# A new order for a fused attention and two-layer MLP kernel: additions placed clear of GpSimd's maxima, small transfers issued by ScalarE

## Chip, cores, metric

One core of one Trainium2 chip. The time is device microseconds of one launch; lower is better. Inputs lie in HBM, the output goes to HBM.

## What is computed

Causal attention over 4 batches x 12 heads x 448 positions x 64 dims, then an MLP on the 1792 x 768 result:

```python
scores = scale * np.matmul(q, k.transpose(0, 1, 3, 2))
scores = np.where(mask, -1000000000.0, scores)
scores = scores - np.max(scores, axis=-1, keepdims=True)
attn = np.exp(scores)
attn = attn / (np.sum(attn, axis=-1, keepdims=True) + 1e-09)
x = np.matmul(attn, v)                   # (4, 12, 448, 64)
x = x.transpose(0, 2, 1, 3).reshape(1792, 768)
h = x @ w_in                             # 768 x 2048
return np.maximum(0.01 * h, h) @ w_out   # 2048 x 768
```

The weights arrive as float64 and are unpacked to float32 on the chip.

## The kernel before

**Attention** runs in 24 units of two heads. For a unit, `qk_load` and `v_load` (issued by SyncE, SP) bring q, k and v; TensorE transposes them (`features`, L421; from unit 12 on VectorE does it, L413), and multiplies keys by queries (`scores`, L450, and the causal mask, L464). A score tile has keys on partitions, so the maximum of softmax runs over partitions: `head` copies chunk 0 to `M` (ScalarE, L479), VectorE takes three elementwise maxima (L264, `M<-S,M`), GpSimd the maximum over partitions (L484, `partition_all_reduce`), VectorE subtracts it chunk by chunk (L489), ScalarE takes the exponential (L496). `products` multiplies by v (L508) and copies the result to `xu` (L514).

**Every second unit `finish` divides.** From batch 1 on VectorE first adds the chunks of each head (three additions `t<-t` per head at L264, turn "add", 108 in all). TensorE sums over keys (L528), ScalarE copies the sums (`sr`, L540), a DMA `sc<-sr` spreads them over 112 partitions ("spread"), VectorE adds 1e-9 and inverts (L543, L544), a DMA `scr<-rc` stores them to HBM ("store"), four DMAs `rb<-scr` broadcast them ("broadcast", issued by ScalarE), and VectorE multiplies (`rb<-xu,rb` or `xf<-xu,rb`) and, for batches 0 and 1, splits x into two parts (ScalarE L261, VectorE `xt<-rb,xt`).

**The MLP.** `layer1` (L602) multiplies batches 0 and 1 by w_in in 576 matmuls; it can start once the x of batch 0 (units 0 to 5) is there, and TensorE weaves it into the attention of later units. Its results go through ScalarE (L607) into one of two buffers `h` and by SP to HBM (`gd<-h`). The weights are unpacked meanwhile: `stage<-in_moe_w_in_dram` by SP, L348, L350 and L370 on ScalarE, L352 and L372 on VectorE. During batches 2 and 3 `ahead` unpacks half of w_out in the same way. After attention `layer1_pair` (L796) and `layer2` (L983) run on TensorE alone.

**Order.** Every operation is recorded with a turn (table `TURN`, one number per kind and unit) and a supposed duration. `Plan.emit` lists them: it takes the engine that is free first, and on it the ready operation with the least turn. The list only sets the order on each engine; the waits on the chip follow from the tiles. Each engine's queue runs in that order, a DMA issue included: an issue that waits holds back all that stands behind it on the engine. Where the plan sees TensorE free it puts warm-up matmuls (L337).

Of the kernel before, what the change touches and what calls it, by code (L numbers as in the profile page):

```python
# [21 lines left out]
    "add": [25.6, 26.6, 27.6, 28.6, 29.6, 30.6, 31.6, 1602.8, 33.6, 1848.1, 35.6, 1480.5, 37.6, 1711.9, 39.6, 1657.6, 41.6, 1656.3, 43.6, 1475.8, 45.6, 1555.1, 47.6, 1436.2],  # L22
    "load": [-2261.1, -2171.6, -2129.4, -2294.2, -2241.4, -2008.9, -1959.9, -1993.3, -1930.3, -2037.5, -2195, -2231.3, -2282, -2312.8, -2224.5, -2161.3, -2231.8, -2175.5, -2242.8, -2255.7, -2117.3, -1991.7, -2075.3, -2074.3],
    "v": [608.6, 652.5, 523.1, 637.8, 734.3, 703.2, 762.6, 586.3, 552.7, 540.9, 645.9, 708.1, 594.1, 649.7, 683.3, 857.5, 861.1, 731.2, 722.3, 719.3, 478.6, 398.8, 556.5, 637.8],
    "transpose": [816, 712.2, 714.5, 763.8, 784.7, 940, 977.5, 999.9, 1298.3, 1281.2, 1210.2, 1393.4, 120.9, 121.9, 122.9, 123.9, 124.9, 125.9, 126.9, 127.9, 128.9, 129.9, 130.9, 131.9],
    "features": [355.5, 270.7, 175.8, 197.8, 329.8, 157.7, 322.1, 351, 391.4, 565.4, 502.8, 597.8, 725.5, 522.1, 546.6, 623, 382.1, 371, 458.7, 236.6, 182.1, 183.3, 171.6, 412.4],
    "scores": [-2016.4, -1926.5, -1879.1, -1903.1, -1875.5, -1837.1, -1727.3, -1731.1, -1837, -1813.4, -1690.1, -1795, -1711.2, -1757.4, -1696.1, -1800.5, -1952.8, -1827, -1903.7, -1725.1, -1882.4, -1895.5, -1928.5, -1800.7],
    "chunk 0": [284.7, 252.5, 434, 449, 448.3, 219.8, 302.8, 386.7, 273.1, 256.8, 189, 193.7, 234.8, 108.9, 159.3, 80, 116.4, -84.5, 28.7, 206.5, 203.1, 222.8, 121, 304.9],
    "max": [-442.1, -415.1, -493, -637, -572.2, -486.9, -543, -585.1, -461.8, -558, -566.8, -672.6, -686.1, -734.9, -552.2, -601.7, -501.7, -450.3, -531.8, -542.6, -594.7, -629.6, -469.8, -416.7],
    "all max": [-1401.3, -1500.2, -1321.8, -1250.4, -1245.6, -1456.8, -1308.5, -1187.8, -1316.5, -1389.6, -1406.9, -1359.6, -1351.7, -1354.9, -1452, -1392.8, -1305.4, -1489.4, -1243.8, -1368.1, -1251.4, -1197.9, -1268.1, -1364.1],  # L30
    "subtract": [3.3, 57.3, 150.1, 102.4, 14.2, 78.1, -59.8, 5.3, 52.2, 67.2, 20.3, 51.6, -222.9, -12.4, -115.4, -84.4, 142.9, 97.4, 198.6, 263.3, 69.9, 170.2, 72.8, 86.1],
    "exp": [-710.2, -914.1, -824.3, -918.4, -801.6, -725.9, -641, -658.2, -777.6, -973.2, -956.7, -1017.4, -1169.2, -1033.8, -996.6, -1022.3, -1081, -957.1, -785.9, -837.9, -834.8, -837.6, -844.2, -736.1],
    "products": [504.4, 609.8, 417.8, 630.3, 514.2, 280.5, 326.3, 302.8, 441.2, 524, 338.2, 416.9, 400.4, 290.3, 306.1, 479.9, 449.6, 568, 460.4, 565.9, 520.1, 509.8, 631.3, 441.2],
# [9 lines left out]
    "out": [140.9, 31.9, -18.1, 33.6, -14, 25.5, 14, 44, 122, 189.5, 211, 171.3, -14.1, 11.2, -68.9, 43.6],
    "xs": [10645.3, 10569.2, 10738.1, 10680.2, 10711.9, 10841.8, 10757.6, 10751.2, 10924, 10924.4, 10920],
    "pair": [10852, 10998.1, 10978, 11043.4, 11022.1, 11050.1, 11075.8, 11360.1],
    "rows": [10737.1, 10610.6, 10696.8, 10778.6, 10751.4, 10772.2, 10635.9, 10692.9, 10658.9, 10721.5, 10679.8, 10681, 10648.9, 10472.9, 10405, 10446.5],
    "product": [-447.4, -613.4, -574.8, -599.2, -666.7, -724.4, -752.5],
    "x lo": [219.3, -457.4, 221.3, -333.8, 223.3, -742.8, 225.3, -349.3, 227.3, -323.9, 229.3, -426, 231.3, -389.5, 233.3, -231.9, 235.3, -265.4, 237.3, -259.8, 239.3, -219.7, 241.3, -253.6],
# [8 lines left out]
PIECE = [1736.3, 1759.7, 1688.7, 1587.5, 1386.6, 1565.0, 1459.4, 1626.7, 1500.3, 1410.5, 1612.2, 1692.9, 1723.9, 1726.6, 1579.9, 1568.4]  # L57


SAME = -365.86  # L60


class Plan:
# [32 lines left out]
    def emit(self, slack, filler):  # L96
# [36 lines left out]
        for _ in range(n):  # L133
# [42 lines left out]
def attention_moe_kernel(  # L176
# [15 lines left out]
    nc = tc.nc  # L192
# [238 lines left out]
    def scores(u):  # L431
# [37 lines left out]
        for e in range(2):  # L469
            head(2 * u + e, e, sl)  # L470
# [607 lines left out]
```

## Time and profile before

| | |
|---|---|
| median of 3 runs | 591.46 us (589.79 to 592.78) |
| the profiled execution | 590.4 us, span 588.6 us |
| TensorE busy | 570.9 us (97%) |
| VectorE busy | 499.6 us (85%) |
| ScalarE busy | 327.8 us (56%) |
| GpSimd busy | 80.5 us (14%) |
| HBM read, written | 99.09 MB, 26.56 MB |

The profile is one execution. PE is TensorE, PEld its weight load, DVE VectorE, ACT ScalarE, POOL GpSimd, SP SyncE; SPq and ACTq are DMA issues on those engines. Busy times of neighbouring instructions on one engine overlap a little, so an engine can be at its limit somewhat below the length of a window.

### The profile page before, as it was taken

Reading aid. Unit: us, or ns where it says so; the run is one execution under the profiler, and the core shown is the slowest. Engines: PE = TensorE matmul, PEld = TensorE weight load, DVE = VectorE, ACT = ScalarE, POOL = GpSimd, SP = SyncE. Lnnn points to the kernel's source line nnn. Section 1 sums busy time; section 2 is a strip of 40 time slices with the busy share of each in tenths; the row PEclk is TensorE's granted clock in tenths of the full one; section 3 lists DMA queues with packets and bytes.
Section 4 is the critical chain, followed back from the end, with each engine's and each line's share of the span. In section 5 each row is a group of like instructions: output and inputs, shape, how many; then the busy total and the mean of one; then the engine's idle time right before and its main releaser. Section 6 shows DMA issues by size and latency. Waiting matters only on the chain.

```text
span 588.6 us, 10664 instructions
## 1 busy us (share of the span) xinstructions
PE 570.9 (97%) x3602; PEld 494.1 (84%) x3602; DVE 499.6 (85%) x1044; ACT 327.8 (56%) x560; POOL 80.5 (14%) x54
## 2 busy tenths in 40 slices
PE   7998899999999999999999999999999999999997
PEld 6666567677777767689999899999999999999997
DVE  4798999999988988966987899899988897888872
ACT  3987797676545666634545775555455544333320
POOL 2443424222423222400000000000000000000000
PEclk9998999999999999999999999999999999999999
DMA  8998678875667898432136996999999997887761
GB/s 174 257 243 193 159 151 253 229 191 122 141 138 199 210 274 257 147 97 94 48 117 203 323 367 219 297 329 303 317 275 281 280 293 202 246 256 230 237 187 52
DMA packets 208967, 126.46 MB, mean 215 GB/s; under 512 B 98832, under 2 KB 202768, under 8 KB 208912
## 3 DMA queue, kind: packets, MB, share of 16 engines
q1 hardware_dynamic: 205072, 120.27, 72.8%
q10 hardware_dynamic: 3840, 5.51, 3.2%
q8 instruction: 28, 0.46, 0.3%
q14 instruction: 27, 0.22, 0.1%
HBM read 99.09 MB, written 26.56 MB: 213 GB/s over the span
## 4 chain that ended last, share of the span: by engine, by line
PE 69%; DMA 12%; DVE 9%; ACT 6%; issue 2%; SPq 2%; POOL 0%; ACTq 0%; DVEq 0%
PE h L983 34%; PE h L796 14%; PE h L602 12%; PE S L450 4%; PE big L508 3%; DMA rb<-scr 2%; DVE t L489 2%; DMA wo<-spare 2%; SPq L258 2%; DMA raw<-in_k_dram 2%; DMA ahead<-in_moe_w_out_dram 1%; DVE t L264 1%; DMA wo<-ahead 1%; ACT t L496 1%; DMA words<-in_moe_w_out_dram 1%
## 5 line engine op out<-in xcount | busy, mean ns | idle before, releaser
L983 PE MATMUL h<-W,r 128*128 128x384 f32 x696 | 127.5, 335 | 0.2
L602 PE MATMUL h<-xt,w 128*128 128x448 f32 x576 | 125.9, 372 | 1.7 <-ACT h L607 1.4
L983 PEld LDWEIGHTS h<-W,r 128*128 128x128 f32 x696 | 121.1, 188 | 0.9 <-ACT r L654 0.4
L602 PEld LDWEIGHTS h<-xt,w 128*128 128x128 f32 x576 | 105.7, 188 | 18.1 <-issue 5.9
L484 POOL PARTITION_ALL_REDUCE MR<-M x48 | 79.9, 1713 | 167.6 <-DVE M L264 120.9
L983 PE MATMUL h<-W,raws 128*128 128x384 f32 x480 | 89.5, 334 | 0.0
L983 PEld LDWEIGHTS h<-W,raws 128*128 128x128 f32 x480 | 83.8, 188 | 0.0
L489 DVE TENSOR_TENSOR t<-S,MR 128x64 f32<-128x64 f32 x192 | 67.6, 415 | 2.0 <-POOL MR L484 1.8
L496 ACT ACTIVATE t<-t 128x1024 f32<-128x1024 f32 x48 | 50.7, 1058 | 18.0 <-DVE t L489 13.3
L264 DVE TENSOR_TENSOR M<-S,M 128x320 f32<-128x320 f32 x144 | 49.1, 353 | 12.6 <-PE S L464 7.2
L450 PE MATMUL S<-kq 64*128 64x64 f32 (+3 forms) x384 | 58.2, 414 | 1.6 <-DVE t L489 1.6
L450 PEld LDWEIGHTS S<-kq 64*128 64x128 f32 x384 | 36.7, 191 | 21.1 <-issue 16.1
L508 PE MATMUL big<-t,v 128*64 128x448 f32 (+3 forms) x384 | 47.2, 386 | 3.5 <-ACT sr L540 1.8
L508 PEld LDWEIGHTS big<-t,v 128*64 128x64 f32 x384 | 26.7, 136 | 25.1 <-issue 10.5
L652 DVE TENSOR_TENSOR v<-A 128x512 f32<-128x512 f32 x70 | 46.6, 694 | 0.0
L654 ACT ACTIVATE r<-v 128x512 fp32r<-128x512 f32 x41 | 24.6, 600 | 37.5 <-DVE v L652 30.6
L264 DVE TENSOR_TENSOR t<-t 128x64 f32<-128x64 f32 (+2 forms) x108 | 39.3, 375 | 2.4 <-PE big L508 0.5
L1011 DVE TENSOR_TENSOR C<-C,h 128x384 f32<-128x384 f32 x56 | 29.1, 550 | 13.3 <-PE h L983 13.3
L655 DVE TENSOR_TENSOR r<-v,r 128x512 fp32r<-128x512 f32 x41 | 28.2, 689 | 8.9 <-ACT r L654 7.6
L654 ACT ACTIVATE W<-v 128x384 fp32r<-128x384 f32 x40 | 19.6, 489 | 27.3 <-DVE v L652 25.0
L654 ACT ACTIVATE raws<-v 128x512 fp32r<-128x512 f32 x29 | 17.4, 601 | 25.6 <-DVE v L652 23.6
L796 PE MATMUL h<-xs,w 128*128 128x448 f32 x144 | 31.6, 366 | 0.0
(108 smaller groups left out, 791.9 us busy)
## 6 DMA issues: line engine op xcount, KB each, us to landing
A<-gd SPq DMA_DIRECT2D x126, 256.0 KB, 4.8
stage<-in_moe_w_in_dram SPq DMA_DIRECT2D x16, 768.0 KB
val<-wo SPq DMA_DIRECT2D x64, 192.0 KB, 4.4
gd<-h SPq DMA_DIRECT2D x51, 224.0 KB, 2.1
ahead<-in_moe_w_out_dram SPq DMA_DIRECT2D x16, 384.0 KB, 4.3
words<-in_moe_w_out_dram SPq DMA_DIRECT2D x16, 384.0 KB, 4.5
val<-wo SPq DMA_DIRECT2D x16, 384.0 KB, 5.3
rb<-scr ACTq DMA_DIRECT2D x48, 112.0 KB, 3.1
```

What stands on the lines that cost most here:

```text
L264: return dve(n, lambda: nc.vector.tensor_tensor(out=out_(), in0=a(), in1=b(), op=op), r, w, prio, **kw)
L450: nc.tensor.matmul(out=T[S_, 2 * e + bank][:, col:col + n], lhsT=T[kq][rows, 128 * c:128 * c + 128], rhs=T[kq][rows, S + qs:2 * S], start= ...
L484: P.op("Pool", 1.75, both(new(mr, p1, [128, S], F32, f"MR{g % 2}"), lambda: nc.gpsimd.partition_all_reduce(T[mr], T[m], 128, ReduceOp.max) ...
L489: f = lambda c=c, qs=qs, n=n: nc.vector.tensor_tensor(out=T[t][:, at(c):at(c) + n], in0=s(c), in1=T[mr][:, qs:], op=ALU.subtract)
L496: act(1024 + 55, lambda: nc.scalar.activation(out=T[t], in_=T[t], func=ACTF.Exp, scale=scale), (), [t], turn("exp", u))
L508: nc.tensor.matmul(out=bigs(key[1])[64 * e:64 * e + 64, qs:S], lhsT=T[vv][:, c, e, :], rhs=T["t", (2 * u + e) % NTB][:, 512 * bank + col:5 ...
L602: nc.tensor.matmul(out=T[key][:, :S], lhsT=T[w, f, 1][:, 128 * c:128 * c + 128], rhs=T["xt", b, x // 3][:, x % 3], start=(c == 0 and j == ...
L652: nc.vector.tensor_tensor(out=x(), in0=get(terms[0]), in1=get(terms[1]), op=ALU.add if terms[2] > 0 else ALU.subtract)
L654: act(n, lambda: nc.scalar.activation(out=hi(), in_=x(), func=ACTF.Copy), [*rd, *hold], [(out_cell, "h")], prio)
L796: nc.tensor.matmul(out=T[key[1]][:, :S], lhsT=wt(o, c), rhs=T["X", x, h][c] if x == "B11" else T["X", x, h][:, c], start=start and c == 0 ...
L983: nc.tensor.matmul(out=T[key][:, :HO], lhsT=g()[:, jj * 128:jj * 128 + 128], rhs=W[:, w * HO:(w + 1) * HO], start=(e == 0 and jj == 0 and ...
L1011: dve(HO, lambda C=C, x=x, sign=sign: nc.vector.tensor_tensor(out=T[C], in0=T[C], in1=x(), op=ALU.add if sign > 0 else ALU.subtract), (), ...
```

## The change

The table of turns is new throughout, and so are `PIECE` and `SAME`. The plan's model is changed: an operation of VectorE that has both inputs in SBUF (marked `cfg=1`) is supposed to shut out GpSimd's maximum and be shut out by it, gets a penalty of 400 in its turn while one runs, and SP's queue is supposed to hold 6.5 us of transfers. Dependencies are recorded per chunk. "spread" and "store" are issued by ScalarE instead of SP, as are the first two q loads; a one-element exponential at the start loads ScalarE's table. Nothing of what is computed changes.

```diff
-    "add": [25.6, 26.6, 27.6, 28.6, 29.6, 30.6, 31.6, 1602.8, 33.6, 1848.1, 35.6, 1480.5, 37.6, 1711.9, 39.6, 1657.6, 41.6, 1656.3, 43.6, 1475.8, 45.6, 1555.1, 47.6, 1436.2],
+    "add": [25.6, 26.6, 27.6, 28.6, 29.6, 30.6, 31.6, 1710.2, 33.6, 1946.1, 35.6, 1528.8, 37.6, 1946.6, 39.6, 1947.6, 41.6, 1955.7, 43.6, 1723.5, 45.6, 1893.7, 47.6, 1693],
...
-SAME = -365.86
+SAME = 384.58
+
+
+DEEP = 6.5
+
+LOCKP = 400
...
-                    key=lambda i: (ops[i][4] - (self.SAME if e == "PE" and ops[i][9] == split else 0.0), i))
+                    key=lambda i: (ops[i][4] - (self.SAME if e == "PE" and ops[i][9] == split else 0.0)
+                                   + (LOCKP if e == "DVE" and ops[i][9] and lock[0] <= t < lock[1] else 0.0), i))
...
+                if e == "DVE" and cfg:
+                    if lock[0] <= t < lock[1]:
+                        t = lock[1]
+                    port = t + us
                 end = free[e] = t + us
+                if e == "Pool" and us > 1:
+                    lock = t + 0.2, max(t + 0.2, port) + 0.74
+                    end = free[e] = lock[1] + 0.7
             if late:
                 dma = max(dma, end + 1.5) + late
+                if e == "SP":
+                    free[e] = max(end, dma - DEEP)
...
+    P.op("ACT", 1.4, lambda: nc.scalar.activation(out=early, in_=ones[:, 0:1], func=ACTF.Exp), ("ones",), ("early",), FIRST)
...
-                loaded[u, tag] = dma(400, lambda key=key: T[key],
-                                     lambda src=src: src[b, 2 * p:2 * p + 2].rearrange("h (s c) d -> s c h d", c=4), [key], [(*key, 0)], turn("load", u))
+                loaded[u, tag] = dma(420, lambda key=key: T[key],
+                                     lambda src=src: src[b, 2 * p:2 * p + 2].rearrange("h (s c) d -> s c h d", c=4), [key], [(*key, 0)], turn("load", u),
+                                     *((0.47, "ACT") if u < 2 and j else ()))
...
-                   (), [("t", g % NTB)], turn("add", u), chain=0.02)
+                   (), [("t", g % NTB)], turn("add", u), cfg=1)
...
-        dma(7, lambda: T[sc], lambda: T[sr][0:97:32, :].rearrange("o (p j) -> o p j", j=16), [sr], [sc], turn("spread", u), 0.68)
+        dma(7, lambda: T[sc], lambda: T[sr][0:97:32, :].rearrange("o (p j) -> o p j", j=16), [sr], [sc], turn("spread", u), 0.53, eng="ACT")
...
-        dma(7, lambda: scr.rearrange("a (p j) -> (a p) j", j=16), lambda: T[rc], [rc], [("scr", u)], turn("store", u))
+        dma(7, lambda: scr.rearrange("a (p j) -> (a p) j", j=16), lambda: T[rc], [rc], [("scr", u)], turn("store", u), 0.53, eng="ACT")
...
-        P.emit({"PE": 0.1, "DVE": 0.1, "ACT": 0.1}, (0.029, "tp", warm))
+        P.emit({"PE": 0.1, "DVE": 0.03, "ACT": 0.1}, (0.029, "tp", warm))
```

What this makes of the order is seen on the engines, at three places. L273 of the changed kernel is L258 of the one before (a DMA), L279 is L264, L512 is L489, L369 is L352.

**The first transfers.** SP's queue before; then SP's and ScalarE's with the change. `raw0` and `raw1` take k and q of even and odd units, `stage` a piece of w_in.

```order
L258 DMA raw0_91<-in_k_dram 112x8x64
L258 DMA raw0_91<-in_q_dram 112x8x64
L258 DMA raw1_93<-in_k_dram 112x8x64
L258 DMA raw1_93<-in_q_dram 112x8x64
L258 DMA v0_92<-in_v_dram 128x3x64 x2
L258 DMA v0_92<-in_v_dram 64x2x64
L258 DMA v1_94<-in_v_dram 128x3x64 x2
L258 DMA raw0_91<-in_k_dram 112x8x64
L258 DMA raw0_91<-in_q_dram 112x8x64
```

```order
L273 DMA raw0_92<-in_k_dram 112x8x64
L273 DMA raw1_94<-in_k_dram 112x8x64
L273 DMA v1_95<-in_v_dram 128x3x64 x2
L273 DMA v1_95<-in_v_dram 64x2x64
L273 DMA v0_93<-in_v_dram 128x3x64 x2
L273 DMA v0_93<-in_v_dram 64x2x64
L273 DMA raw0_92<-in_k_dram 112x8x64
L273 DMA stage_119<-in_moe_w_in_dram 128x6x256
L273 DMA raw0_92<-in_q_dram 112x8x64
```

```order
L273 DMA raw0_92<-in_q_dram 112x8x64
L273 DMA raw1_94<-in_q_dram 112x8x64
L316 ACT_TABLE_LOAD
L316 ACTIVATE early_89<-ones_87 128x1
L443 ACTIVATE kq_0_132<-big_90 128x448
```

The k of unit 1 is now SP's second transfer, not its third; q of units 0 and 1 are ScalarE's first; the first piece of w_in goes ahead of the q of unit 2.

**ScalarE's queue at the second division** (units 2 and 3; `sr` holds the sums). With the change, from the issue of "spread" to the first "broadcast":

```order
L273 DMA sc_0_120<-sr_0_769 112x1x16
L498 ACTIVATE M_1_797<-S_711 128x448
L517 ACTIVATE t_3_606<-t_3_606 128x1024
L367 ACTIVATE stage_119<-stage_119 128x768
L536 ACTIVATE xu_0_817<-big_91 128x448
...
L273 DMA scr3_99<-rc_0_860 112x16
L498 ACTIVATE M_1_874<-S_803 128x448
L517 ACTIVATE t_4_767<-t_4_767 128x1024
L517 ACTIVATE t_5_768<-t_5_768 128x1024
L443 ACTIVATE kq_0_906<-big_90 128x448
L387 ACTIVATE w_908<-stage_119 128x768
L273 DMA rb_0_121<-scr3_99 64x448 x2
```

Before, the first and the seventh of these rows stood in SP's queue, and ScalarE's had M, two exponentials and one kq ahead of the broadcasts. Now both wait and are waited for in ScalarE's own queue.

**VectorE's queue in batch 3**, from the last subtractions of one unit to the first of the next; first before, then with the change:

```order
L264 TENSOR_TENSOR M_0_2604<-S_2571,M_0_2604 128x320
L264 TENSOR_TENSOR M_0_2604<-S_2571,M_0_2604 128x192
L264 TENSOR_TENSOR M_0_2604<-S_2569,M_0_2604 128x64
L264 TENSOR_TENSOR M_1_2608<-S_2572,M_1_2608 128x320
L264 TENSOR_TENSOR M_1_2608<-S_2572,M_1_2608 128x192
L264 TENSOR_TENSOR M_1_2608<-S_2570,M_1_2608 128x64
L352 SCALAR_TENSOR_TENSOR ahead_2267<-ahead_2267,ahead_2266 128x384
L264 TENSOR_TENSOR t_2_2518<-t_2_2518 128x64
L352 SCALAR_TENSOR_TENSOR spare1_96<-spare1_96,spare0_95 128x384
L543 TENSOR_SCALAR sc_0_116<-sc_0_116 112x16
L544 RECIPROCAL rc_0_2646<-sc_0_116 112x16
L489 TENSOR_TENSOR t_4_2654<-S_2569,MR_0_2622 128x64
```

```order
L279 TENSOR_TENSOR M_0_2681<-S_2645,M_0_2681 128x320
L279 TENSOR_TENSOR M_0_2681<-S_2645,M_0_2681 128x192
L369 SCALAR_TENSOR_TENSOR spare1_97<-spare1_97,spare0_96 128x384
L279 TENSOR_TENSOR M_0_2681<-S_2643,M_0_2681 128x64
L279 TENSOR_TENSOR M_1_2689<-S_2646,M_1_2689 128x320
L279 TENSOR_TENSOR t_2_2554<-t_2_2554 128x64
L279 TENSOR_TENSOR M_1_2689<-S_2646,M_1_2689 128x192
L279 TENSOR_TENSOR t_2_2554<-t_2_2554 128x192
L279 TENSOR_TENSOR M_1_2689<-S_2644,M_1_2689 128x64
L512 TENSOR_TENSOR t_4_2552<-S_2643,MR_0_2705 128x64
```

Before, an addition and two unpackings stood between the last maximum of both heads and the first subtraction; now one unpacking stands ahead of M_0's last maximum, and the additions among the maxima of the second head.

## Rows read from the trace of the kernel before

**Rows 1.** Busy time in stretches of core 0: stretch, length, engines, clock, DMA.

```profile
0.00:20.00 20.00, 16.74 (x211) 13.33 (x213) 10.25 (x43) 10.39 (x16) 4.39 (x9) 1.00 0.92 207
20.00:45.00 25.00, 23.23 (x228) 15.46 (x224) 23.14 (x58) 22.44 (x37) 12.48 (x8) 1.00 1.01 242
45.00:70.00 25.00, 19.95 (x166) 13.22 (x165) 21.94 (x56) 18.72 (x30) 10.08 (x6) 0.93 0.70 153
70.00:100.00 30.00, 30.00 (x215) 21.85 (x214) 28.63 (x68) 26.45 (x40) 7.18 (x6) 1.00 0.86 220
100.00:125.00 25.00, 24.53 (x153) 18.07 (x153) 24.04 (x54) 17.36 (x25) 6.50 (x4) 1.00 0.86 232
125.00:200.00 75.00, 74.93 (x519) 55.54 (x515) 68.50 (x180) 42.42 (x70) 23.07 (x14) 1.00 0.65 153
200.00:250.00 50.00, 47.52 (x311) 35.86 (x308) 43.14 (x113) 32.20 (x58) 16.77 (x10) 1.00 0.77 224
```

**Rows 2.** The chain that ended last: start us, us, what.

```profile
259.83 16.93 PE h L602 x81
...
276.76 40.32 PE h L796 x198
```

**Rows 3.** Timeline, 0 to 20 us: start, us, engine, line, operation, idle before.

```profile
2.24 0.69 SPq L258 DMA_DIRECT2D raw<-in_k_dram  x1
...
12.06 0.60 PE L421 MATMUL big<-ident,raw 112*128 112x112 f32 x4 [1.49 <-DMA raw<-in_k_dram]
...
14.44 0.54 ACT L424 ACTIVATE kq<-big 128x448 f32<-128x448 f32 x1
...
15.04 1.71 PE L337 MATMUL big<-warmb 128*128 128x64 bf16 x53 [0.25 <-ACT kq L424]
...
17.75 1.14 PE L450 MATMUL S<-kq 64*128 64x448 f32 x8
```

**Rows 4.** DMA issues by tile: count, duration ns min/median/max.

```profile
L258 SPq DMA_DIRECT2D sc<-sr x12: 587/598/798, 28.8 to 260.5; - x12
L258 SPq DMA_DIRECT2D scr<-rc x12: 325/364/541, 35.5 to 263.0; - x12
```

**Rows 5.** Timeline, second division, 52 to 60 us.

```profile
52.42 0.35 SPq L258 DMA_DIRECT2D scr<-rc  x1
...
57.43 2.40 ACTq L258 DMA_DIRECT2D rb<-scr  x4
...
59.88 0.84 ACT L370 ACTIVATE w<-stage 128x768 fp32r<-128x768 f32 x1 [2.82 <-DMA rb<-scr]
```

**Rows 6.** Timeline, third division, 61 to 65 us.

```profile
61.18 0.61 SPq L258 DMA_DIRECT2D sc<-sr  x1
...
64.36 0.25 DVE L544 RECIPROCAL rc<-sc 112x16 f32<-112x16 f32 x1
```

**Rows 7.** Timeline, GpSimd maxima and additions of VectorE near 212 and 238 us.

```profile
210.51 3.34 POOL L484 PARTITION_ALL_REDUCE MR<-M  x2 [7.06 <-DVE M L264]
...
212.30 0.95 DVE L264 TENSOR_TENSOR t<-t 128x64 f32<-128x64 f32 x1
...
238.55 0.22 DVE L264 TENSOR_TENSOR t<-t 128x64 f32<-128x64 f32 x1
```

**Rows 8.** Groups by form: busy us, mean ns of one.

```profile
L264 DVE TENSOR_TENSOR M<-S,M 128x64 f32<-128x64 f32 x48 | 10.8, 225 | 1.7
...
L264 DVE TENSOR_TENSOR t<-t 128x64 f32<-128x64 f32 x36 | 10.1, 280 | 0.5 <-PE big L508 0.5
```

**Rows 9.** Timeline, SP, ScalarE and TensorE, 210 to 215 us.

```profile
210.32 0.59 SPq L258 DMA_DIRECT2D sc<-sr  x1
...
210.97 1.11 SPq L258 DMA_DIRECT2D gd<-h  x2
...
214.22 1.15 ACT L607 ACTIVATE h<-h 128x448 f32<-128x448 f32 x2 [0.81 <-DMA gd<-h]
...
214.82 3.31 PE L602 MATMUL h<-xt,w 128*128 128x448 f32 x15 [1.36 <-ACT h L607]
```

More of the change, by code (lines that the diff above doesn't have):

```diff
@@ L43 @@
[L43 to L47, printed above, removed]
@@ new lines @@
+    "take sums": [-520.8, -219.1, -518.8, -175.2, -516.8, -278, -514.8, -206.4, -512.8, -161.6, -510.8, -204.3, -508.8, -227.6, -506.8, 120.6, -504.8, -320.3, -502.8, -4.6, -500.8, 120.2, -498.8, -278.5],
+    "spread": [15.1, 28.2, 17.1, 112.3, 19.1, 97.7, 21.1, -2.4, 23.1, 140, 25.1, 153.9, 27.1, 4.1, 29.1, -67, 31.1, 242.3, 33.1, 411.9, 35.1, 204.7, 37.1, 30.8],
+    "invert": [145.6, -373, 147.6, -299.4, 149.6, -231.7, 151.6, -160.2, 153.6, -442.7, 155.6, -149, 157.6, -481.2, 159.6, -625.2, 161.6, -579.9, 163.6, -702.1, 165.6, -411, 167.6, -620.4],
@@ L415, in features @@
             return
+        P.op("X", 0.0, new(kq, keep if u % 2 else p1, [128, 2 * S], F32, f"kq{u % 2}"), w=[kq, (*kq, 0), (*kq, 1)], prio=turn("features", u))
         for j, tag in enumerate(("kraw", "qraw")):
@@ L424, in features @@
             f = lambda j=j, tp=tp: nc.scalar.activation(out=T[kq][:, j * S:(j + 1) * S].rearrange("p (s c) -> p s c", c=4), in_=bigs(tp[1])[:, 0:S].rearrange("p (c s) -> p s c", c=4), func=ACTF.Copy)
-            if j == 0:
-                f = both(new(kq, keep if u % 2 else p1, [128, 2 * S], F32, f"kq{u % 2}"), f)
-            act(S + 55, f, [], [tp, kq, (*kq, j)] if j == 0 else [tp, (*kq, j)], turn("features", u), give=tp)
+            act(S, f, [kq], [tp, (*kq, j)], turn("features", u), give=tp)
     order = sorted(segs)
@@ L468, in scores @@
                turn("scores", u), rows=120, cfg=1)
-        for e in range(2):
-            head(2 * u + e, e, sl)
+        todo = [head(2 * u + e, e, sl) for e in range(2)]
+        for h in todo:
+            for _ in h:
+                pass
     def head(g, e, sl):
@@ L489, in head @@
             f = lambda c=c, qs=qs, n=n: nc.vector.tensor_tensor(out=T[t][:, at(c):at(c) + n], in0=s(c), in1=T[mr][:, qs:], op=ALU.subtract)
-            if c == 3:
-                f = both(new(t, p1, [128, 1024], F32, "t%d" % t[1]), f)
             last = max(n for n in range(2 * EARLY) if n % 3 == 2)
             gives = ("mm", ("S", sl[2 * e + bank])) if 2 * u + bank == last and c in (0, 1) else None
-            dve(n, f, [mr], [t, bk(c)], turn("subtract", u), give=gives)
-        act(1024 + 55, lambda: nc.scalar.activation(out=T[t], in_=T[t], func=ACTF.Exp, scale=scale), (), [t], turn("exp", u))
+            before = dve(n, f, [mr, bk(c), t], [(t, c)], turn("subtract", u), give=gives, after=() if gives is None else (before,))
+        yield
+        act(1024 + 55, lambda: nc.scalar.activation(out=T[t], in_=T[t], func=ACTF.Exp, scale=scale), [(t, c) for c in order], [t], turn("exp", u))
+        yield
     NTB = 6
@@ L513, in products @@
            [key], turn("products", u), rows=120, cfg=2, take=key)
-        act(S + 55, both(new(xu, p1, [128, S], F32, f"xu{u % 3}"), lambda: nc.scalar.activation(out=T[xu], in_=bigs(key[1])[:, 0:S], func=ACTF.Copy)),
+        act(S, both(new(xu, p1, [128, S], F32, f"xu{u % 3}"), lambda: nc.scalar.activation(out=T[xu], in_=bigs(key[1])[:, 0:S], func=ACTF.Copy)),
             [key], [xu], turn("take products", u), give=key)
```

97 lines of the change are left out of this document (52 added, 45 removed).

## Prediction, made before the changed kernel was run

> **What bounds the kernel now.** I read the busy times by stretch first, because the engines' shares of the whole run hide that the stages differ. The reader should see three stages [rows 1]. From 0 to 70 us TensorE has only attention to do and stands still for 3.26 us in the first 20, 1.77 in the next 25 and 5.05 in the 25 after that, 10.1 us together. From 70 to 200 us it is filled with layer 1 matmuls: idle 0.00, 0.47 and 0.07 us. From 200 to 250 us it loses 2.48 us again. Then the chain that ended last: after the last sums 81 matmuls of layer 1 run without a break, 16.93 us or 209 ns each, and the next product runs on at once [rows 2]. From there to the end TensorE is never short of work.
>
> The work on TensorE is the same before and after but for warm-up matmuls. So the change can win only what TensorE loses before 250 us, 12.6 us by these rows, and it can lose if it adds a wait there. VectorE and ScalarE are the other two limits in the first stage: 23.14 and 22.44 of 25 us between 20 and 45 us [rows 1]. A saving on one of them counts only where the other is not full.
>
> The profiled execution took 590.4 us, 1.06 below the median of the runs; I make the sum against 590.4 and carry the difference over to the median of 591.46.
>
> **The change part by part.**
>
> *First loads (term A).* TensorE waits 1.49 us at 12.06 us for the k of unit 2 [rows 3]. In SP's queue one issue fewer stands ahead of it, and one fewer ahead of the k of unit 1: an issue takes 0.69 us [rows 3]. ScalarE issues the q loads at a time when it has nothing else to do, since 10.39 of its first 20 us are all it works. I take -0.7 us, ends 0 and -1.5. Against it: the first piece of w_in (a sixteenth of 768 x 2048 float64, 786 KB) now stands ahead of the q of unit 2. At the 207 GB/s of this stretch it takes 3.8 us [rows 1]. The cover is that unit 2's features were ready at 14.98 (14.44 + 0.54) and its scores began only at 17.75, so 2.8 us are free [rows 3]; with the 0.7 us from the shorter queue, 3.5 of the 3.8 are covered, and I book nothing.
>
> *58 more warm-up matmuls.* The order has 178, before 120. A run of 53 took 1.71 us, 32 ns each [rows 3], so they are 1.9 us of TensorE, put where the plan sees it wait. 168 of them stand ahead of the first product with v, before 113. I book 0, ends 0 and +1.9.
>
> *Issues on ScalarE (term B).* Twelve "spread" at 0.60 us and twelve "store" at 0.36 us move from SP to ScalarE, 11.5 us in all [rows 4]. After 70 us ScalarE has room (17.36 of 25 us and less from 100 us on) and TensorE has other work. Before 70 us there are three of each, 2.9 us, and ScalarE is full between 20 and 45 us [rows 1]. I take +1.0 us, as one of the three divisions falls into the full stretch; ends 0 and +2.9.
>
> *The round trip of the reciprocals (term C).* At the second division "store" is issued at 52.42, and the broadcast that needs it goes out only at 57.43, 5.0 us later; ScalarE, behind that issue in its queue, stands idle for 2.82 us [rows 5]. This is in the stretch in which TensorE loses most, 5.05 us [rows 1]. SP issues other transfers around it; the DMA engines are busy 70% of this stretch and all of the one before [rows 1]. In ScalarE's queue the store stands behind no bulk load. I take -2.0 us, ends 0 and -5.05. The rule that speaks against this: the Trainium skill, page "DMA: Bandwidth & Descriptors", section "Issuing engines are not separate DMA queues", says that transfers of all issuing engines run interleaved on the same 16 DMA engines and that spreading them saves issue time alone. By the rows the store came late with a busy SP, which does not tell a queue from a bandwidth; by the rule C would be 0 and the time 2.0 us longer. It is a rival below.
>
> *Additions and maxima (term D).* An addition of 128x64 took 0.95 us at 212.30, beside GpSimd's maxima of 210.51 to 213.85; another of the same size took 0.22 at 238.55 [rows 7]. So a place beside a maximum can cost 0.73 us. Over the run the 36 small additions average 280 ns where maxima of that size average 225 [rows 8]: 55 x 36 = 2.0 us is what the additions lose in all. In the new order they still stand near the maxima, but ahead of the last one of the second head. I take -0.7 us, one stall, since in most of the run TensorE does not wait for VectorE; ends 0 and -2.0. The Trainium skill, page "SBUF — State Buffer", section "Who interferes with whom", says an operation of VectorE with two inputs in SBUF and one of GpSimd that reads SBUF shut each other out for the whole instruction. The rows disagree on the length: 0.73 us, not a whole maximum of 1.67 (3.34 / 2). By the rule one stall would be worth 1.67 us and the sum 0.9 lower.
>
> *SP's queue (term E).* At 210.32 SP issues "spread", behind loads, and only then the two stores of layer 1's results. ScalarE waits 0.81 us for that store to free a buffer, and TensorE 1.36 us for ScalarE [rows 9]. With "spread" and "store" gone from SP such a hold is shorter. I take -1.8 us of the 2.48 lost between 200 and 250 us [rows 1], ends 0 and -2.5.
>
> *The rest of the order.* From 70 to 200 us TensorE loses 0.54 us, so there is nothing to win and a new hole is possible. I book 0, ends -0.5 and +3.
>
> Sum: -0.7 + 0 + 1.0 - 2.0 - 0.7 - 1.8 = **-4.2 us**: 586.2 against the profiled execution, **587.3** against the median. What is late next in each place: after C, VectorE (21.94 of 25 us in that stretch); after E, the sums and exponentials of the last units.
>
> **The rivals.**
>
> *ScalarE waits in its own queue (slower).* "Store" on ScalarE waits for VectorE's reciprocal, and all that stands behind it waits too. From the issue of "spread" to the end of the reciprocal the third division took 3.4 us (61.18 to 64.61) [rows 6]. At the second division the new order puts far more than that between the two issues, so it is covered there; elsewhere an M and two exponentials, some 2.7 us, are all there is. If the three early stores wait 1.5 us each and term B counts whole, ScalarE loses 4.5 + 2.9 = 7.4 us before 70 us, C brings nothing, and A, D and E give back 3.2: +4.2, or 595.7 us. It decides from the point where ScalarE's loss before 70 us is over 3.2 us. For it: ScalarE is at 22.44 of 25 us there. Against it: the cover at the second division.
>
> *The landing is no sooner (no change).* If the store was late because the DMA engines were full, C is 0: 589.3 us. For it: they were full from 20 to 45 us. Against it: 70% when the store ran. That is the time by the Trainium skill's rule on issuing engines above.
>
> *VectorE holds the pace anyway (no change).* It is busy 23.14, 21.94 and 28.63 us of 25, 25 and 30 up to 100 us [rows 1], and its work is unchanged. Then A, B, C and E all end in front of a full VectorE, and only D, which is VectorE's own, remains: 590.8 us. Against it: 5.05 us of TensorE idle beside 3.06 of VectorE means that both wait for a third.
>
> *The additions are not clear of the maxima (no change).* The new rows still have them ahead of subtractions. D is then 0, and one more stall takes 0.7: -4.2 + 0.7 + 0.7, or 588.7 us.
>
> *More is won.* If the stretch from 45 to 70 us closes wholly (C at -5.05), E is -2.5 and A -1.5, the sum is -9.5 with D at -1.5 and B at 1.0: 582 us.
>
> **How the numbers follow.** Forecast 0.44, more won 0.14: faster by over 0.5% (under 588.5; half a per cent is about what a measurement of this kernel can tell from no change), 0.58. Landing no sooner 0.12, VectorE's pace 0.12, additions not clear 0.04: within 0.5%, 0.28. ScalarE's own waits 0.14: slower. The range runs from 582 to 594: it leaves out a part of the last case and what lies under 582, and the ends of A to E and of new holes lie inside it.
>
> **What would show it.** C right: from "store" to the first broadcast clearly under 5.0 us at the second division, and TensorE busy over 21.5 of 25 us there. B right: ScalarE's idle time ended by VectorE's reciprocal under 1 us for the first three stores. D right: small additions near 225 ns. E right: under 1 us of TensorE's waits between 200 and 250 us for ScalarE's L607. A right: no 1.49 us wait for the k of unit 2. The prediction is wrong if TensorE's idle time before 250 us stays at 12 us, or if it loses time after 280 us, for which no row gives a reason.

## The result, and the profile after

The changed kernel took **596.99 us** (median of 13 runs, 593.82 to 599.96), the kernel before 592.73 in the runs beside it (13, 588.83 to 597.04): ratio **1.0079**, 95% interval 1.0051 to 1.0108. It is slower by 0.8%; the forecast was 587.3, the range ended at 594. The profiled execution took 597.85 us, its span 596.0, 7.4 above the span before. That is more than the 4.3 us between the medians: the profile before lies 2.3 us under its median, the changed one 0.9 over.

Busy time by stretch, changed kernel, columns as in [rows 1]:

```profile
0.00:20.00 20.00, 17.24 (x254) 14.47 (x256) 9.57 (x40) 10.22 (x17) 3.72 (x8) 1.00 0.95 202
20.00:45.00 25.00, 20.86 (x210) 13.36 (x210) 21.09 (x54) 22.21 (x34) 10.63 (x7) 1.00 0.95 213
45.00:70.00 25.00, 20.88 (x186) 13.02 (x176) 20.76 (x58) 18.88 (x31) 10.55 (x7) 0.93 0.70 166
70.00:100.00 30.00, 28.26 (x199) 19.93 (x196) 28.24 (x67) 24.10 (x37) 9.91 (x6) 1.00 0.84 202
100.00:125.00 25.00, 25.00 (x168) 17.93 (x165) 24.73 (x60) 18.01 (x27) 7.96 (x4) 1.00 0.77 197
125.00:200.00 75.00, 74.73 (x491) 56.56 (x488) 63.42 (x165) 42.14 (x68) 21.94 (x14) 1.00 0.68 165
200.00:250.00 50.00, 49.96 (x323) 37.55 (x322) 42.46 (x113) 32.20 (x56) 14.68 (x9) 1.00 0.87 244
sum 250.00, PE 236.93 PEld 172.82 DVE 210.27 ACT 167.76 POOL 79.37; mean PE 33.85 PEld 24.69 DVE 30.04 ACT 23.97 POOL 11.34
```

Against [rows 1], 200 to 250 us is now full (49.96 of 50; 47.52 before), but 20 to 45 us lost 2.4 us and 70 to 100 us 1.7. TensorE is idle for 13.1 us of the 250, exactly as before: the idle time moved from a late place to an early one. So idle time does not show the loss. Counting matmuls in the two traces does, by milestones (us from the start of the span):

| | before | changed | late by |
|---|---|---|---|
| first score matmul | 7.6 | 8.8 | 1.2 |
| transposes of the eighth unit | 44.6 | 47.3 | 2.7 |
| 37th matmul of layer 1 | 85.8 | 90.5 | 4.7 |
| last matmul of layer 1 | 276.4 | 281.3 | 4.9 |
| first matmul of layer 2 | 380.0 | 388.5 | 8.5 |

So there are two losses: nearly 5 us in the first 90, and 3.6 in the two-stack layer (`layer1_pair`, L818), which took 107.0 us in place of 103.4. That stage is in no term of the prediction. Behind it 1.1 us come back: the last matmul of layer 2 ends 204.0 us after its first, 204.8 before, and what follows takes 3.5 us in place of 3.8.

Up to the 37th matmul of layer 1 both kernels do the same matmuls but for the warm-ups. Counting each one up to the start of the next, 2.7 of the 4.7 us there are more idle time and 1.8 are 54 more warm-ups. From there to the last matmul of layer 1 nothing is won: 190.6 us before, 190.9 with the change, though idle time falls from 3.1 to 0.4 us. The sums over keys take 10.8 us in place of 9.1, the causal masks 6.5 in place of 4.9; why they take longer is not shown. Sums and warm-ups from the start to the last matmul of layer 1 (count, busy us, mean ns of one, idle before), before:

```profile
L528 PE MATMUL big<-t,ones 128*32 128x448 f32 (+3 forms) x168 | 15.6, 455 | 0.6 <-DVE t L264 0.5
L337 PE MATMUL big<-warmb 128*128 128x64 bf16 x120 | 6.9, 215 | 1.5 <-DVE place L267 1.0 <-DVE row L307 0.2 <-ACT kq L424 0.2
```

and with the change:

```profile
L550 PE MATMUL big<-t,ones 128*32 128x448 f32 (+3 forms) x168 | 17.4, 460 | 1.7 <-ACT kq L443 1.7
L354 PE MATMUL big<-warmb 128*128 128x64 bf16 x178 | 8.8, 210 | 1.2 <-DVE place L282 1.0 <-DVE row L324 0.2
```

The longest wait of the first loss, in the timeline of the changed kernel from 25 us (start, us, engine, line, operation, idle before):

```profile
25.32 0.86 ACT L387 ACTIVATE w<-stage 128x768 fp32r<-128x768 f32 x1
...
27.12 0.91 ACT L365 ACTIVATE stage<-stage 128x768 f32<-128x768 f32 x1 [0.94 <-DMA stage<-in_moe_w_in_dram]
27.94 1.04 ACT L517 ACTIVATE t<-t 128x1024 f32<-128x1024 f32 x1
28.88 0.96 ACT L443 ACTIVATE kq<-big 128x448 f32<-128x448 f32 x2
...
29.46 1.93 PE L550 MATMUL big<-t,ones 128*32 128x448 f32 x32 [1.71 <-ACT kq L443]
```

and at the same place of the work before:

```profile
24.36 1.07 ACT L496 ACTIVATE t<-t 128x1024 f32<-128x1024 f32 x1
25.30 0.99 ACT L424 ACTIVATE kq<-big 128x448 f32<-128x448 f32 x2
...
25.92 1.93 PE L528 MATMUL big<-t,ones 128*32 128x448 f32 x32
26.15 0.98 ACT L348 ACTIVATE stage<-stage 128x768 f32<-128x768 f32 x1
```

Before, ScalarE unpacked a w_in piece (L348) after it had copied q and k out of the PSUM buffer that the sums need. Now the piece (L365) stands ahead, waits 0.94 us for its load, and TensorE waits 1.71 us at the sums. In a second execution of the changed kernel this wait is 0.6 us and the 37th matmul of layer 1 is at 91.7 us, so this wait alone does not make the loss.

One wait of the second, in the timeline of the changed kernel from 341 us:

```profile
341.67 0.55 ACT L365 ACTIVATE vals<-words 128x384 f32<-128x384 f32 x1 [3.14 <-DMA words<-in_moe_w_out_dram]
...
342.69 0.56 DVE L369 SCALAR_TENSOR_TENSOR vals<-vals 128x384 int32<-128x384 int32 x1 [1.95 <-ACT vals L367]
...
344.30 0.61 DVE L830 TENSOR_TENSOR h<-s,h 128x448 f32<-128x448 f32 x1
...
344.97 1.28 PE L818 MATMUL h<-xs,w 128*128 128x448 f32 x5 [1.55 <-DVE h L830]
```

A w_out row lands late, VectorE's unpacking waits for it, the addition behind it frees a buffer late, and TensorE waits 1.55 us.

### The profile page after: what moved, and what is told of

It reads as the page before. It is cut to its first block, busy times and chain, and to the rows that moved or that the text cites. A ratio compares the mean times of both kernels' runs of the same rounds, so it can differ in the third digit from the quotient of the medians.

```text
span 596.0 us, 10755 instructions
## 1 busy us (share of the span) xinstructions
PE 577.0 (97%) x3660; PEld 496.5 (83%) x3660; DVE 494.8 (83%) x1044; ACT 329.2 (55%) x561; POOL 83.1 (14%) x54
## 4 chain that ended last, share of the span: by engine, by line
PE 72%; DMA 10%; DVE 10%; ACT 5%; issue 2%; POOL 1%; SPq 0%; ACTq 0%; DVEq 0%; POOLq 0%
PE h L1005 34%; PE h L624 18%; PE S L467 7%; PE big L530 5%; PE h L818 4%; DMA words<-in_moe_w_out_dram 3%; DVE F L794 3%; DMA stage<-in_moe_w_in_dram 2%; PE big L550 2%; DMA rb<-scr 2%; DMA raw<-in_q_dram 1%; DVE xs L737 1%; ACT t L517 1%; DVE h L830 1%; DVE S L805 1%
## 5 line engine op out<-in xcount | busy, mean ns | idle before, releaser
L505 POOL PARTITION_ALL_REDUCE MR<-M x48 | 82.6, 1757 | 173.0 <-DVE M L279 141.6
L512 DVE TENSOR_TENSOR t<-S,MR 128x64 f32<-128x64 f32 x192 | 67.7, 411 | 4.6 <-POOL MR L505 4.3
L467 PE MATMUL S<-kq 64*128 64x448 f32 (+3 forms) x384 | 59.6, 411 | 0.5 <-DVE t L512 0.4
L279 DVE TENSOR_TENSOR M<-S,M 128x320 f32<-128x320 f32 (+2 forms) x144 | 43.6, 347 | 10.8 <-PE S L481 6.5
L674 DVE TENSOR_TENSOR v<-A 128x512 f32<-128x512 f32 x70 | 47.6, 692 | 0.8 <-DMA A<-gd 0.6
L1033 DVE TENSOR_TENSOR C<-C,h 128x384 f32<-128x384 f32 x56 | 30.7, 548 | 12.1 <-PE h L1005 12.0
L279 DVE TENSOR_TENSOR t<-t 128x64 f32<-128x64 f32 (+2 forms) x108 | 37.8, 390 | 0.4
L818 PE MATMUL h<-xs,w 128*128 128x448 f32 x144 | 32.4, 370 | 2.2 <-DVE h L830 1.5
L818 PE MATMUL h<-xs,S 128*128 128x448 f32 x144 | 31.7, 368 | 0.4 <-DVE g L830 0.4
```

The costliest lines, as they stand in the source:

```text
L279: return dve(n, lambda: nc.vector.tensor_tensor(out=out_(), in0=a(), in1=b(), op=op), r, w, prio, **kw)
L467: nc.tensor.matmul(out=T[S_, 2 * e + bank][:, col:col + n], lhsT=T[kq][rows, 128 * c:128 * c + 128], rhs=T[kq][rows, S + qs:2 * S], start= ...
L505: P.op("Pool", 1.75, both(new(mr, p1, [128, S], F32, f"MR{g % 2}"), lambda: nc.gpsimd.partition_all_reduce(T[mr], T[m], 128, ReduceOp.max) ...
L512: f = lambda c=c, qs=qs, n=n: nc.vector.tensor_tensor(out=T[t][:, at(c):at(c) + n], in0=s(c), in1=T[mr][:, qs:], op=ALU.subtract)
L674: nc.vector.tensor_tensor(out=x(), in0=get(terms[0]), in1=get(terms[1]), op=ALU.add if terms[2] > 0 else ALU.subtract)
L818: nc.tensor.matmul(out=T[key[1]][:, :S], lhsT=wt(o, c), rhs=T["X", x, h][c] if x == "B11" else T["X", x, h][:, c], start=start and c == 0 ...
```

## Experiments

All versions compute the whole reference. In most the plan's list is written out as numbers of operations, so that a queue's order can be put together from both kernels; the waits still follow from the tiles. The lines are those of the changed kernel. Each ratio is to runs of the kernel before that were made beside that version; their medians lie between 590.44 and 592.73 us, so versions are best compared by ratio.

```diff
     def emit(self, slack, filler):
-        ops, n = self.ops, len(self.ops)
...
-        for f in order:
-            f()
+        ops, pools, slot = self.ops, self.pools, self.slot
+        for n, i in enumerate(ORDER):
...
+            ops[i][2]()
```

### Order or issuing engine

```diff
-        dma(7, lambda: T[sc], lambda: T[sr][0:97:32, :].rearrange("o (p j) -> o p j", j=16), [sr], [sc], turn("spread", u), 0.53, eng="ACT")
+        dma(7, lambda: T[sc], lambda: T[sr][0:97:32, :].rearrange("o (p j) -> o p j", j=16), [sr], [sc], turn("spread", u), 0.53, eng="SP")
```

and the same for "store" and the first q loads: the changed order with all issues on SP ("after_sp"). "before_act" is the reverse, the order before with these issues on ScalarE.

> The changed kernel with its order of instructions kept, but the first q loads and the small transfers of the sums and reciprocals issued by SyncE again, at their places in the order. Theory O (the order of the start and of the two-stack first layer costs the 4 to 5 us, the issuing engine next to nothing): 595.5 to 598.5 us, no better than the changed kernel. Rival I (the issues on ScalarE cost it: the first q loads land late, and ScalarE is held by its issues): 594 us or less, and the first score matmul near 7.6 us instead of 8.8.

Measured 598.95 us, ratio to before 1.0109 (1.0068 to 1.0150): 0.45 us over Theory O's range, and nowhere near Rival I's 594. The first score matmul did come early, at 7.9 us, and that won nothing.

> The kernel before with its order of instructions kept, but the first q loads and the small transfers of the sums and reciprocals issued by ScalarE. Theory O: within 1 us of the kernel before, 592 to 594 us. Rival I: 595.5 us or more, and ScalarE idle before it copies products or sums near the divisions.

Measured 593.65, ratio 1.0013 (0.9983 to 1.0044). The issuing engine is worth nothing that can be told from zero; the order is worth the loss. The order also fills the stretch from 200 to 250 us. "after_sp":

```profile
200.00:250.00 50.00, 49.80 (x330) 38.10 (x329) 42.58 (x113) 32.00 (x56) 13.52 (x9) 1.00 0.88 243
```

and "before_act":

```profile
200.00:250.00 50.00, 46.91 (x332) 34.18 (x330) 43.64 (x114) 32.56 (x59) 14.01 (x9) 1.00 0.82 240
```

The stretch is full with the changed order though SP issues everything, and not full with ScalarE's issues in the old order.

### Where in the order

"start_before" takes the order before up to 95 us of its plan, then the changed one; "first45" and "first20" switch at 45 and 20 us, "start125" at 125; "after45" has the order before only between 45 and 95 us. "after_pair" goes back to the order before for everything after the attention, "start_pair" for both ends.

In short, not the code itself:

```diff
-ORDER = changed
+ORDER = before[: 95 us] + [i for i in changed if i not in before[: 95 us]]
```

> The order of the kernel before up to its planned 95 us (first q loads from SyncE), then the order of the changed kernel; sums and reciprocals by ScalarE throughout. Theory O: it wins back the 4.5 us that TensorE has lost by 92 us and keeps the 3.5 us of loss in the two-stack layer: 592 to 593.5 us. If the loss at the start is made up later anyway (another wait takes its place): 596 us or more.

Measured **589.81**, ratio 0.9945 (0.9918 to 0.9972): faster than both kernels, 7 us under the changed one, and under Theory O's range, which kept a loss in the two-stack layer that did not stay (103.8 us). Among what the first 95 us bring back is the old number of warm-ups: this version has 125, the changed kernel 178. Its stretches:

```profile
20.00:45.00 25.00, 23.03 (x226) 15.09 (x224) 23.15 (x59) 22.59 (x37) 12.26 (x8) 1.00 1.00 224
45.00:70.00 25.00, 20.41 (x185) 12.91 (x182) 23.31 (x62) 20.03 (x33) 11.24 (x7) 1.00 0.78 178
70.00:100.00 30.00, 29.08 (x210) 20.90 (x209) 28.09 (x67) 25.99 (x40) 6.63 (x4) 1.00 0.88 215
...
200.00:250.00 50.00, 49.67 (x337) 36.95 (x334) 43.49 (x111) 33.24 (x60) 15.35 (x10) 1.00 0.77 228
```

The start is nearly back at what it was (23.03 and 29.08; 23.23 and 30.00 before), and 200 to 250 us stays full.

> The order of the changed kernel up to the end of the attention, then the order of the kernel before for the two-stack first layer and the second layer. Theory O: the 3.5 us that the two-stack layer lost (281 to 388 us) come back: 593 to 594 us, and the last matmul of that layer follows its first by 103.4 us as before, not by 106.9. If the loss there is only what the late start hands on, or was chance: 596 us or more.

Measured 594.54, ratio 1.0040 (1.0017 to 1.0062), between the two forecasts; the two-stack layer took 104.2 us in the profile.

> The changed kernel itself once more, for the length of its two-stack layer. If the 3.5 us of loss there belong to its order: from first to last matmul 106.5 to 107 us again. If they come and go with the landing of the w_out words: 103.4 to 104.5 us, as in the five other profiles of that order there.

In this second execution the layer took 104.7 us (one time, 595.86). So 2.3 of the 3.6 us came and went between two executions of one program; what the other 1.3 hang on is not shown. Over all profiles the changed order took 103.4 to 107.0 us in this stage (14 profiles; 106.8 and more in the first one of the changed kernel, in "loads" and in "pieces", which the expectation above leaves out), the order before 102.8 to 104.3 (6 profiles). The first loss stayed: last matmul of layer 1 at 281.7, with TensorE idle for only 11.1 of the first 250 us.

> Three pieces: the order of the kernel before up to its planned 95 us, that of the changed kernel from there to the end of the attention, that of the kernel before for the two-stack first layer and the second layer. If the start and the two-stack order are two separate losses: 587 to 588 us, 2 us under the version with the start alone (589.8). If the time of the two-stack layer varies by chance and not by its order: 589 to 590.5 us.

Measured 591.17, ratio 0.9980 (0.9951 to 1.0010): over both ranges, and nothing on top of the start alone. Behind the changed start the old late order is 2.3 us faster (1.0079 to 1.0040), behind the old start 2.1 us slower (0.9945 to 0.9980). The intervals overlap both times, so no run shows a fixed worth of that order.

> The order of the kernel before only up to its planned 45 us (first q loads from SyncE), then that of the changed kernel. If the loss arises in the first loads and first w_in pieces (theory: crowded start): 590 to 592 us, nearly all of what the version with 95 us won. If it arises at the divisions and at the first layer-1 work after 45 us: 594.5 us or more.

Measured 592.43, ratio 1.0028 (1.0000 to 1.0055): just over the first range. By ratio the first 45 us bring back 3.0 of the 7.9 us that 95 us bring (1.0079, 1.0028, 0.9945), so not nearly all.

> The order of the kernel before on all engines up to its planned 20 us (first q loads from SyncE), then that of the changed kernel. With 45 us so replaced the time was 592.4 us, with 95 us 589.8, against 597.0 of the changed kernel. If the loss of the first 45 us is made by the first loads and transposes: 592 to 593.5 us. If it is made at 20 to 45 us (unpacking of w_in pieces among the copies of q and k): 595.5 us or more.

Measured 594.62, ratio 1.0036 (1.0008 to 1.0065), between the forecasts, but in its profile the last matmul of layer 1 came at 281.2, no earlier than in the changed kernel (281.3); with 45 us it came at 277.6, with 95 at 276.3. This version has 123 warm-ups, so without the 55 others its profile is late all the same. The warm-ups were not tried by themselves.

> The order of the changed kernel up to its planned 45 us, that of the kernel before from there to its 95 us, then that of the changed kernel. If the losses before and behind 45 us are separate and add up: 594 to 595.5 us (the 2.6 us between the versions with 45 and with 95 us off 597.0). If the order before fits only its own start: 597 us or more. If the loss lies behind 45 us alone: 590 to 592 us.

Measured 596.51, ratio 1.0069 (1.0043 to 1.0096), last matmul of layer 1 at 281.9. Once the first 45 us are the changed ones, the old order behind them saves nothing that can be told from zero. So the losses before and behind 45 us do not add up.

> The order of before up to its planned 125 us, then the changed one. If the changed order gains between 95 and 125 us: slower than the version with 95 us (589.8), 590 to 592 us. If its gain lies behind 125 us: 589 to 590 us.

Measured 602.22, ratio 1.0178 (1.0144 to 1.0213): outside both ranges. The same two orders, joined 30 us later, cost 12 us more. Its TensorE waits from 95 to 150 us:

```profile
PE S L467 <- DVE t L512: 3.0, 2, 2.4
PE big L550 <- DVE t L279: 2.7, 1, 2.7
```

The join itself can cost more than anything that it is meant to measure, so a version that loses says little about the part that was put back. One that wins shows that the parts fit better than those they replace.

### Which part of the start

Put back into the changed order: the loads of the first 45 us ("loads"), the first five w_in pieces ("pieces"), the first three ("pieces3"), loads and three pieces ("loads_pieces3"), ScalarE's and VectorE's queues to 95 us ("act_dve"), TensorE's and SP's ("pe_sp").

In short:

```diff
-ORDER = changed
+ORDER = changed, with these operations at the times that the plan before gave them
```

> The changed kernel, with only the loads of the first 45 us (q, k, v and w_in pieces, all from SyncE) in the order that they had before; every computing engine keeps the changed order. Theory L (v and w_in loads issued ahead of the q and k loads of the next units make those land late): 592.5 to 594.5 us, first score matmul at 7.6 to 8 us. If the loads are innocent: 596 to 598 us.

598.19, ratio 1.0125 (1.0083 to 1.0167): no gain.

> The changed kernel, with only the loads and the unpacking of the first w_in pieces (SyncE, ScalarE, VectorE) moved back to the places that they had in the order before, 2 to 5 us later. Theory P (a piece's unpacking stands ahead of the copies of q and k in ScalarE's queue and waits there for its load, and TensorE with it): 592.5 to 594.5 us and the 1.7 us wait of TensorE for the copy of q and k at 29 us gone. If the pieces are innocent: 596 to 598 us.

601.13, ratio 1.0164 (1.0125 to 1.0202): slower than either forecast. In its profile the longest wait at the sums fell to 1.0 us, but one of 3.3 us for the copy of products and one of 2.2 us for that of q and k came in its place.

> The changed kernel with only the first three w_in pieces (load, unpacking, split) moved back to their places of before, 1 to 10 us later, and nothing else. Theory P (these unpackings stand ahead of the copies of q and k and hold ScalarE for a load): 592 to 594.5 us, without the new collisions behind 30 us that moving five pieces brought. If their place does not matter: 596 to 598 us. If it matters only together with the loads: 596 us or more here, and less with both.

597.60, ratio 1.0095 (1.0064 to 1.0126): no gain.

> Both together: the loads of the first 45 us in the order of before, all from SyncE, and the first three w_in pieces' unpacking at its places of before; the rest in the changed order. If the crowded loads and the unpackings that wait for them are one cause: 592 to 594 us, with TensorE busy for 9 us or more of 20 to 30 us. If the start only fits as a whole: 597 us or more.

599.58, ratio 1.0135 (1.0094 to 1.0175): no gain from both together.

> The changed kernel, with ScalarE's and VectorE's queues in the order that they had before among all the work planned ahead of 95 us (w_in pieces, copies of q and k, exponentials, subtractions, divisions together); TensorE and SyncE keep the changed order. Theory Q (the start is lost in these two queues as a whole: what stands behind an operation that waits for a load is late, and TensorE with it, and moving the pieces alone only shifted the collision): 590 to 593 us. Rival T (TensorE's own changed order of 64 to 95 us and the load order cost it): 596 us or more.

611.09, ratio 1.0333 (1.0302 to 1.0363): against Theory Q.

> The complement: TensorE's and SyncE's queues in the order that they had before among the work planned ahead of 95 us (first q loads from SyncE too), ScalarE and VectorE in the changed order. Theory Q: 595 to 599 us. Rival T: 590 to 593 us. If neither this nor its complement wins, the loss comes from queues that fit each other only as a whole.

604.36, ratio 1.0225 (1.0190 to 1.0261): against Rival T too.

None wins, and both halves of the start alone are worse than either whole. That the queues fit each other only as a whole is the reading that is left; it is not shown, since every mixture also adds waits of its own. Parts were then added to the order before:

> The kernel before, with only the loads of its first 45 us (q, k, v, w_in pieces, all from SyncE) put into the changed order; every computing engine as before. In profiles with the start of before the 57th transpose starts at 44.5 to 46.3 us, in those with the changed start at 47.3 to 48.9. If the changed order of the loads is enough to make the start late: 47 us or more there and 594.5 us or more in all. If the loads are innocent: 592 to 593 us.

600.16, ratio 1.0177 (1.0138 to 1.0216); transposes of the eighth unit at 54.3 us. TensorE's waits to 75 us begin

```profile
PE big L440 <- DMA raw<-in_k_dram: 5.1, 3, 3.9
PE S L467 <- DVE t L512: 2.4, 5, 0.6
PE big L440 <- DMA raw<-in_q_dram: 2.1, 1, 2.1
```

> The kernel before, with only the first three w_in pieces (load, unpacking, split) at the earlier places of the changed order. If a piece's unpacking ahead of the copies of q and k is enough to make the start late: the 57th transpose at 47 us or later and 594.5 us or more. If the pieces are innocent: 592 to 593 us.

595.71, ratio 1.0074 (1.0042 to 1.0106); eighth unit at 47.6 us. Each part alone is enough to make the old start late. By the same token neither is shown to be what makes the changed start late: with its loads alone the old order is 1.8% slower, more than twice the loss of the changed kernel.

## Why the prediction was wrong

**Rest of the order: 0, ends -0.5 and +3. This step failed.** It looked for a new hole between 70 and 200 us, since TensorE stood idle there least, and took the start as a place where time could only be won. The runs put about 7 us on the order of the first 95 us, its warm-ups included (596.99 against 589.81). In the profiles 5.0 us are there at the last matmul of layer 1 (281.3 against 276.3 us), and 3.7 of these belong to the first 45 us (277.6); by the times the first 45 us are worth less than half, so that split is rough. Some of the 5.0 us is clock: from 45 to 70 us the mean granted clock was 0.93 in the changed kernel and 1.00 in "start_before", which I estimate at up to 1.8 us (7% of 25 us). The rest of the distance between these two profiles is the two-stack layer (107.0 against 103.8), whose order is the same in both. No rival had this case: the slower one was ScalarE waiting in its own queue for its issues, and "before_act", which has these issues, is at 1.0013.

A premise failed with it: that the work on TensorE is the same, so that only its idle time can be won or lost. The rows give 13.1 us of idle time before 250 us (the 12.6 leave out 70 to 200 us), the changed kernel has 13.1 as well, and it is 5 us late.

**A, -0.7, with a w_in piece ahead of the q of unit 2 booked at nothing.** The wait of 1.49 us for the k of unit 2 is gone, as forecast, but up to 92 us TensorE now waits 2.0 us for a q, three times, and the longest comes earlier:

```profile
8.26 0.61 PE L440 MATMUL big<-ident,raw 112*128 112x112 f32 x4 [1.19 <-DMA raw<-in_q_dram]
```

TensorE's order now has the transposes of the q of unit 1 ahead of those of its k, and the first scores stand behind them. That q is ScalarE's second issue and lands late. The first score comes at 8.8 us (8.6 to 9.5 in the four profiles that start so); at 7.9 in "after_sp" (SP's q lands in time) and at 7.9 in "before_act" (ScalarE's q loads, but k first). It takes the order and the issuing engine together, and I had read the two apart. But it is not the loss: "after_sp" does not have this wait and is at 1.0109. The piece itself costs little where I looked: the other two waits for a q are 0.3 and 0.5 us. But I counted the slack of one unit, while a piece moves the loads of every unit behind it, and its unpacking moves in ScalarE's queue. What that can cost is seen in "before_loads", with the loads in the changed order and the engines as before: TensorE waits 3.9 us at once for a k.

**Warm-ups, 0.** The holes did not get fewer: 1.8 us of warm-ups up to the 37th matmul of layer 1, beside 2.7 us more of idle time. The upper end, +1.9, was the nearer one in this profile.

**B, +1.0.** Together with C and E as far as they hang on the issuing engine, the measured sum is +0.8 us (0.13%, interval -0.17 to +0.44), where 1.0 - 2.0 - 1.8 was forecast. The sign that was named came true: the three early stores go out at 38.93, 55.18 and 67.67 us, each within 0.04 us of the reciprocal's end, and no idle time of ScalarE is put down to it. So the slower rival, ScalarE waiting in its own queue, did not happen there.

**C, -2.0.** The round trip did fall, 3.70 us from "store" to the broadcast, against 5.01 [rows 5]:

```profile
55.18 0.33 ACTq L273 DMA_DIRECT2D scr<-rc  x1
...
58.88 0.47 ACTq L273 DMA_DIRECT2D rb<-scr  x1
```

but TensorE is busy 20.88 of 25 us there, under the 21.5 named. And the mechanism was wrong: with the changed order and SP's store ("after_sp") the round trip is 3.68 us,

```profile
57.17 0.61 SPq L273 DMA_DIRECT2D scr<-rc  x1
...
60.85 0.45 ACTq L273 DMA_DIRECT2D rb<-scr  x1
```

and with the old order and ScalarE's store ("before_act") it is 4.56. So it hangs on the order, not on SP's queue, and at the third division it got longer (1.84 before, 3.11 with the change). The idle 2.82 us of ScalarE were misread too: from 57.43 on, 2.40 of them are the issuing of the four broadcasts [rows 5], which no earlier landing shortens. The Trainium skill, page "DMA: Bandwidth & Descriptors", section "Issuing engines are not separate DMA queues", says that another issuing engine saves issue time alone; the time of "before_act" agrees (1.0013).

**D, -0.7: wrong in sign.** The additions did not come clear of the maxima. Additions by form, busy us and mean ns, changed kernel:

```profile
L279 DVE TENSOR_TENSOR t<-t 128x192 f32<-128x192 f32 x36 | 13.7, 402 | 0.0
L279 DVE TENSOR_TENSOR t<-t 128x64 f32<-128x64 f32 x36 | 9.4, 283 | 0.1
```

and before:

```profile
L264 DVE TENSOR_TENSOR t<-t 128x192 f32<-128x192 f32 x36 | 12.8, 356 | 1.0
```

The small ones stayed at 283 ns ([rows 8]: 280), those of 192 rose from 356 to 402. 40 of the 108 additions now run beside a maximum, 22 before. Only 7 of them are longer for it, 3 before; against the undisturbed ones they lose 4.5 us, 2.2 before. It is not what decides: "start_before" has 7 long ones too, 4.5 us. (One stall of 1.67 us in place of 0.7 would have put the sum 1.0 us lower, not 0.9 as I wrote.)

**E, -1.8: the wait went, the time did not.** 47.52 became 49.96, and TensorE's wait for ScalarE's L607 is gone, as the sign named for E asked. But with SP's issues back it is 49.80, so the order of the work filled the stretch and not a shorter queue; what in that order did it was not tried. And in this pair of profiles the filling won no time, as the milestones show: 190.6 us from the 37th to the last matmul of layer 1 before, 190.9 with the change.

**The test named for failure** came true: TensorE's idle time before 250 us stayed at 13.1 us, and time was lost after 280 us.

What stays open: which of the waits of the start begins the delay, how much of it the added warm-ups are, why sums and masks take longer behind it, and why the w_out rows land late in some executions of the two-stack layer.

## What to carry to other kernels

Where every engine's queue is fixed by one list, a change of the list is not the sum of the moves that its diff shows: price it also at the stage whose buffers and loads are tightest, even if that stage has idle time to spare; here that idle time was waiting and not room. Do not take idle time for progress: count when the same piece of work is reached in both traces. To find a loss in such a change, swap whole stretches of all queues in time and keep what wins; here, moving one kind of work or one engine's queue mostly measured the misfit. An issue moved to another engine should be measured by itself, with the order held.

## What the runs showed of the hardware

A version that fits badly can cost clock too. "act_dve", stretches with the granted clock in the third column from the end:

```profile
70.00:100.00 30.00, 22.89 (x136) 15.78 (x135) 21.79 (x52) 15.13 (x23) 7.18 (x4) 0.84 0.64 147
100.00:125.00 25.00, 22.31 (x122) 17.01 (x121) 16.22 (x38) 16.94 (x26) 6.33 (x4) 0.85 0.46 130
```

TensorE stands idle for 7.1 and 2.7 us of these stretches, and part of their time ran at the lower of its two levels, 1.2 in place of 2.4 GHz; in the kernel before, the mean from 70 to 250 us was 1.00 [rows 1].

An addition beside a GpSimd maximum is not always longer; it depends on where in the maximum it starts. In the two traces 9 of the 10 long additions start 0.14 to 0.35 us after the beginning of a maximum (0.87 to 1.09 us long). Of the 52 others beside one, all start before it, in its first 0.02 us, or 0.79 us or more behind its beginning, and they take their undisturbed 0.2 to 0.5 us. The tenth long one, of 0.72 us, starts 0.98 us into a maximum that itself took 2.29 us.
